# One attention and MoE kernel: the values' 16-bit parts are made in the bias stage and stored

## The chip, the core and the metric

The kernel runs on one core of a Trainium2 chip. The metric is the device time of one execution in microseconds (us). Before the change the median of three runs is 802.57 us (799.44 to 804.67).

## What is computed

Attention with a bias that comes from a small network on positions, then a gated feed-forward layer without routing ("MoE" in the code) on its output:

```python
scores = scale * np.matmul(q, k.transpose(0, 1, 3, 2))      # 4 batches, 8 heads, 576 x 576, head_dim 64
x = (log1p(|i - j|) / log1p(max(i, 1)))[..., None]
bias = np.maximum(x @ w1 + b1, 0.0) @ w2                     # 32 hidden, one bias per head
attn = softmax(scores + bias)
x = np.matmul(attn, v)  as [2304 tokens, 512]
out = (sigmoid(x @ w_gate) * (x @ w_val)) @ w_out            # d_ff 1536
```

All inputs and outputs are float32. The kernel keeps the accuracy with products of parts: a number is written as a high part and the rest, and a product as two or three matmuls of parts.

## The kernel before

**Bias stage** (`bias`, some 14 to 112 us). The bias is made per chunk of 64 query columns, nine chunks `c`. TensorE sums switches (`ind`, `far`) times coefficients into `bps` (L427); each chunk has five blocks of rows in the order `BORD` = 0, 1, 4, 2, 3, called groups here, number `5c + n`. `leave` takes a group out of PSUM: VectorE multiplies one half by `xt` into `btmp` (L435, L448), ScalarE copies the other half to `brest` for blocks 0 and 4 (L438), and the sum is made by VectorE (L443) or, for blocks 0 and 4, by GpSimd (L443, L453). `btmp`, `brest` and `bps` have two buffers each. The switches of the next chunk are made meanwhile: TensorE's L403 from a loaded table `lt` and ScalarE's L408, and VectorE's comparison L421, whose operands both lie in SBUF. VectorE and ScalarE also reformat weights for the MoE (`conv`, L225 to L237: load of `cvw`, store of `cvm`).

For the attention the values `v` are split to two 16-bit parts after a scaling by a power of two. The scale comes from the sum of squares of `v`: per batch a load of `vb` on GpSimd's queue (L458), 20 matmuls (`gram`, L350) in block 4 of chunks 3 to 6, two VectorE operations; and in chunk 7 one `fit` for all batches (L364 to L378), nine small VectorE operations and a matmul.

**Attention** (`attention`, some 110 to 372 us). There are 16 units `u`, one for a pair of heads `p` and a batch `b`. A unit has nine slots `s`. In even slots TensorE makes the scores of two tiles (L627; slot 8: one tile, L616), VectorE adds the bias and takes the minimum (L643, `mn`), ScalarE takes the exponential (`en`, L648). Two slots later (`LAG`) a tile is turned: those of head 0 by TensorE (L672, L679; then ScalarE L561 and VectorE L562 write high part and rest to `at`), those of head 1 (`CROSS`) by GpSimd, which writes both parts to `cr` (L555, L666), and a transposing DMA (L667), which is issued `XLAG` = 3 slots after. `cr` has three buffers. The last columns are turned by `tail` in slot 3 of the next unit. In each unit's slots 0 to 8 TensorE also does 0, 6, 3, 6, 3, 6, 3, 6, 3 matmuls (`FILL`) of the last unit's `products`, from slot 2 on: four groups of nine matmuls (L732), one for each head `h` and half `e` of the query columns, into the one buffer of `acc`; ScalarE copies a group to `xe` (L736), of which there are two, and when both halves of a head are there, SP stores it to `xs` (L741). `split_v` makes the two parts of the values in slots 5 and 7: ScalarE L602 and VectorE L603 on `vr`, which SP loaded (L548). VectorE's L696 scales the softmax sums for a store to `rs`.

The order of the instructions on each engine is that in which the program writes them: both stages run under a manual schedule. Each engine, and each DMA queue (almost all of it SP's), works in that order; an instruction that waits holds up those behind it.

**MoE** (`Moe`, from 372 us on, with loads and conversions in the last units of the attention). The change does not touch it.

## Time and profile before

| | |
|---|---|
| median of three runs | 802.57 us |
| the profiled execution, its own time | 800.84 us |
| its span, first to last instruction | 799.0 us |
| granted TensorE clock, mean | 0.987 of full speed |
| busy share TensorE / VectorE / ScalarE / GpSimd | 92% / 81% / 70% / 45% |
| bias stage, attention, MoE (from the trace, roughly) | 14 to 112, 110 to 372, 372 to 799 us |

In the trace PE is TensorE (PEld its weight loads), DVE VectorE, ACT ScalarE, POOL GpSimd, SPq and ACTq DMA queues. L732 is line 732 of the kernel's file. "x12" counts instructions, "<-" in a tile name reads "written from", and behind a row stands the engine's idle time before it and what ended that.

### The profile page before, as it was taken

The numbers are of one execution on the slowest core, as the hardware profiler recorded it, in microseconds if no ns is written. First come the engines' busy times: TensorE is split into PE (matmuls) and PEld (weight loads), VectorE is DVE, ScalarE is ACT, GpSimd is POOL, SyncE is SP. The second block draws the span as 40 slices with busy tenths as digits, with TensorE's granted clock in tenths as the row PEclk, the third lists the DMA queues.
The fourth block names the chain that finished last, engine by engine and source line by source line (L and its number), as shares of the span: only waits on it lengthen the run. The fifth ranks groups of instructions, "written<-read, shape, count | busy, mean of one in ns | idle before, by whom it ended". The sixth has DMA issues, their size and how long they took to land. (4 is left out here: it accounts for less than half of the span.)

```text
span 799.0 us, 17293 instructions
## 1 busy us (share of the span) xinstructions
PE 735.8 (92%) x6343; PEld 539.5 (68%) x6343; DVE 650.3 (81%) x1362; ACT 555.4 (70%) x1206; POOL 360.1 (45%) x451
## 2 busy tenths in 40 slices
PE   7999879888888988777999999998999999999997
PEld 4898867666766766565899899974555555555553
DVE  6788879888888889996498998878988886877762
ACT  5888738787887878776666666577666667666652
POOL 2245349788879986973001110046733221533100
PEclk9999988999999999999999999999999999999999
DMA  5487315878888798898989863357522211422102
GB/s 199 149 202 175 116 59 119 190 181 168 178 174 186 184 185 208 204 220 207 320 259 257 260 172 107 108 148 190 175 80 80 80 53 57 155 80 80 54 1 80
DMA packets 137237, 121.86 MB, mean 153 GB/s; under 512 B 82368, under 2 KB 106048, under 8 KB 137152
## 3 DMA queue, kind: packets, MB, share of 16 engines
...
## 5 line engine op out<-in xcount | busy, mean ns | idle before, releaser
L1158 PEld LDWEIGHTS <-wv 128*128 128x128 f16 x1008 | 98.0, 98 | 85.5 <-issue 10.7
L648 ACT ACTIVATE en<-en,mn 128x576 f32<-128x576 f32 x144 | 110.8, 774 | 24.7 <-DVE mn L643 22.6
L1116 POOL TENSOR_TENSOR ws<-wm 128x256 f32<-128x256 f32 x44 | 42.4, 964 | 157.2 <-DMA wm<-scratch 109.0
L1158 PE MATMUL pg<-xq,wv 128*128 128x384 f16 x576 | 109.3, 326 | 3.3 <-ACT c L1184 2.4
L643 DVE CUSTOM_DVE_ANT_0 en<-sc,bias 128x576 f32<-128x576 f32 x128 | 91.9, 755 | 21.5 <-PE sc L627 19.1
L732 PE MATMUL acc<-at,vv 128*128 128x288 f16 x540 | 84.1, 288 | 19.4 <-DVE at L562 10.7
L666 POOL TENSOR_TENSOR cr<-en,cr 128x512 f16<-128x512 f32 (+1 forms) x128 | 97.1, 779 | 5.3
L627 PEld LDWEIGHTS sc<-k,part 64*128 64x128 f32 x768 | 58.5, 189 | 43.1 <-DVE mn L643 16.5
L627 PE MATMUL sc<-k,part 64*128 64x288 f32 x768 | 78.3, 317 | 10.0 <-DVE mn L643 8.1
L1005 PE MATMUL po<-wo,gh 128*128 128x512 f16 x288 | 85.7, 379 | 0.0
L1158 PE MATMUL pu<-xq,wv 128*128 128x384 f16 x432 | 82.0, 326 | 2.1 <-DVE c L1164 2.1
...
L1164 DVE TENSOR_TENSOR c<-pu,c 128x384 f32<-128x384 f32 x72 | 40.0, 555 | 42.5 <-PE pu L1158 28.7
L562 DVE SCALAR_TENSOR_TENSOR at<-pt,at 128x512 f16<-128x512 f32 (+3 forms) x128 | 69.5, 564 | 5.8 <-ACT at L561 4.8
L561 ACT ACTIVATE at<-pt 128x512 f16<-128x512 f32 (+3 forms) x128 | 60.1, 496 | 19.9 <-PE pt L672 19.8
L732 PEld LDWEIGHTS <-vv 128*128 128x128 f16 x576 | 56.2, 98 | 25.0 <-issue 9.3
L427 PE MATMUL bps<-cfs,ind 128*128 128x64 bf16 x1458 | 67.5, 193 | 3.5 <-DVE bias L443 1.8
L408 ACT ACTIVATE ind<-y 128x576 bf16<-128x576 f32 x100 | 62.4, 651 | 10.8 <-PE y L403 8.0
L427 PEld LDWEIGHTS <-ind 128*128 128x128 bf16 x1458 | 58.7, 98 | 9.7 <-issue 3.0
L555 POOL TENSOR_SCALAR cr<-en 128x576 f16<-128x576 f32 x64 | 45.3, 708 | 43.9 <-DMA at<-cr 32.8
L1176 ACT ACTIVATE gh<-c 128x384 f16<-128x384 f32 x48 | 25.1, 523 | 54.1 <-DVE c L1174 52.5
L672 PE MATMUL pt<-ident,en 128*128 128x128 f32 x320 | 53.3, 291 | 6.5 <-ACT en L648 6.4
...
## 6 DMA issues: line engine op xcount, KB each, us to landing
...
```

Source lines behind the costliest of these rows:

```text
L408: nc.scalar.activation(out=o, in_=y[:, :, 0:HF], func=AF.Sigmoid, scale=float(2.0 ** 64))
L427: nc.tensor.matmul(out=o, lhsT=st, rhs=cfs[:, part], start=(part == 0), stop=(part == 2))
L561: nc.scalar.activation(out=hi, in_=ps, func=AF.Copy, scale=float(2.0 ** UP))
L562: return lambda: nc.vector.scalar_tensor_tensor(out=lo, in0=ps, scalar=float(2.0 ** UP), in1=hi, op0=ALU.mult, op1=ALU.subtract)
L627: nc.tensor.matmul(out=pair[h][:, e, 0:HF], lhsT=qs[rows, l, 128 * it:128 * it + 128], rhs=ks[rows, r, HF * e:HF * e + HF], start=(i == 0) ...
L643: nc.vector.tensor_tensor_reduce(out=half(en), in0=ps[:, :, 0:HF], in1=half(nbias), scale=-0.125, scalar=3.0e38, op0=ALU.add, op1=ALU.min, ...
L648: nc.scalar.activation(out=en, in_=en, func=AF.Exp, bias=mn, scale=-1.0, accum_out=sm)
L666: nc.gpsimd.tensor_tensor(out=t[:, a:a + z.stop - z.start], in0=en[:, z], in1=t[:, z], op=ALU.subtract)
L672: nc.tensor.transpose(pt[:, J], en[:, 128 * J:128 * J + 128], ident)
L732: nc.tensor.matmul(out=acc[:, 0:HF], lhsT=l, rhs=r, start=(i == 0), stop=(i == len(mms) - 1))
L1005: self.nc.tensor.matmul(out=po, lhsT=l[:, tt], rhs=r, start=(first and i == 0), stop=(last and i == 2))
L1158: nc.tensor.matmul(out=p, lhsT=W[i][:, l, at + kc], rhs=V[b][:, r, kc], start=(new and n == 0), stop=(n == 5), skip_group_check=not new)
```

## The change

The values' parts are made in the bias stage, by GpSimd, and stored in DRAM (`vs`, one tensor per unit); the attention loads them ready-made (`vv`, in slot 2). The scale is now one per batch. `vb` is loaded from the start on, `gram` stands in block 4 of chunks 0 to 3, and a `fit` for the batch of the chunk before in chunks 1 to 4. From group 8 on (chunk 1, fourth group) `parts` and its `rest` are called in turn, once per group: scale in place and round to the high part, then the low part by subtraction, the store of `vs` and the load of the next `vr` but one on SP. `split_v` leaves the attention. The scaling of the softmax sums moves from VectorE to ScalarE. `products` runs over column halves outside and heads inside; `cr` has four buffers; the transposing DMA is issued two slots after the turn instead of three.

```diff
-LAG, WSTEP, VSTEP, TAIL = 2, 2, (5, 7), 3
+LAG, WSTEP, VSTEP, TAIL = 2, 2, 2, 3
...
-XLAG = 3
+XLAG = 2
...
-VCHUNK = (3, 4, 5, 6, 7)
+VSTART = 7
...
+    vs = [dram.tile([128, 2, 5, 2, D], F16, name=f"vs{i}") for i in range(B * NP)]
...
+        rp, op = pool("vraw", 2), pool("vparts", 2)
         squares = cp.tile([128, B], F32, name="vsq")
...
+        most = cp.tile([128, B], BF16, name="vmost")
+        size = [level.tile([128, B], F32, name=n) for n in ("vnorm", "vup", "vun", "vout")]
+        sizes.update(out=size[3], tiny=sm[:, 2 * HID + 17 + H:2 * HID + 26 + H])
+        vb, vr, ready = [], [], []
+        nc.gpsimd.memset(ones, 1.0)
...
+        def load_vr(n):
+            t = rp.tile([128, 2, 5, D], F32, name="vr")
+            nc.sync.dma_start(out=t, in_=v[n // NP, n % NP])
+            vr.append(t)
...
+                nc.vector.tensor_copy(out=most[:, n:n + 1], in_=squares[:, n:n + 1])
...
+        def fit(ps, n):
+
...
+            a = slice(n, n + 1)
+            o = ps.rearrange("p a h j -> p (a h j)")[:, 128:129]
+            nc.tensor.matmul(out=o, lhsT=ones, rhs=most[:, a], start=True, stop=True, skip_group_check=True)
...
             def leave():
-                m, up, un = (t.bitcast(I32) for t in size[0:3])
+                m, up, un = (t[:, a].bitcast(I32) for t in size[0:3])
                 e = nc.vector
-                e.tensor_scalar(out=size[0], in0=o, scalar1=float(2.0 ** -80), scalar2=None, op0=ALU.max)
...
-                e.tensor_tensor(out=size[3], in0=size[2], in1=sm[:, 2 * HID + 26 + H:], op=ALU.mult)
+                e.tensor_tensor(out=size[3][:, a], in0=size[2][:, a], in1=sm[:, 2 * HID + 26 + H:], op=ALU.mult)
...
+        def parts(n):
+
...
+            b, p = divmod(n, NP)
+            t, o = vr.pop(0), op.tile([128, 2, 5, 2, D], F16, name="vparts")
+            hi, lo = o[:, :, :, 0], o[:, :, :, 1]
+            nc.gpsimd.tensor_scalar(out=t, in0=t, scalar1=size[1][:, b:b + 1], scalar2=1.0, op0=ALU.mult, op1=ALU.mult)
+            nc.gpsimd.tensor_scalar(out=hi, in0=t, scalar1=1.0, scalar2=1.0, op0=ALU.mult, op1=ALU.mult)
+
+            def rest():
+                nc.gpsimd.tensor_tensor(out=lo, in0=t, in1=hi, op=ALU.subtract)
+                nc.sync.dma_start(out=vs[B * p + b], in_=o)
+                if n + 2 < B * NP:
+                    load_vr(n + 2)
+
+            return rest
+
+        for n in range(2):
+            load_vb(n)
...
-                late = None
-                if blk == 4 and c in VCHUNK:
-                    at = VCHUNK.index(c)
-                    late = gram(ps[:, 1], at) if at < B else fit(ps[:, 1])
-                    if at + 1 < B:
-                        load_vb(at + 1)
-                if blk == 4 and c == VCHUNK[0] - 1:
-                    load_vb(0)
+                late = []
+                if blk == 4 and c < B:
+                    late.append(gram(ps[:, 1], c))
+                    if c + 2 < B:
+                        load_vb(c + 2)
+                if blk == 4 and 0 < c <= B:
+                    late.append(fit(ps[:, 1], c - 1))
                 leave(ps, c, blk)
-                if late:
-                    late()
+                for f in late:
+                    f()
+                if (c, n) == (0, 4):
+                    for i in range(2):
+                        load_vr(i)
+                z = 5 * c + n - VSTART - 1
+                if ready:
+                    ready.pop()()
+                elif 0 <= z and z // 2 < B * NP:
+                    ready.append(parts(z // 2))
...
-    def load_v(u):
-        p, b = units[u]
-        vraw[u] = raw.tile([128, 2, 5, D], F32, name="vr")
-        nc.sync.dma_start(out=vraw[u], in_=v[b, p])
...
-    crp = pool("crp", 3)
+    crp = pool("crp", 4)
...
-    def split_v(u, h):
-        if h == 0:
-            vsplit[u] = vp.tile([128, 2, 5, 2, D], F16, name="vv")
-        t, vv = vraw[u][:, h], vsplit[u][:, h]
-        nc.scalar.activation(out=vv[:, :, 0], in_=t, func=AF.Copy, scale=sizes["up"])
-        return lambda: nc.vector.scalar_tensor_tensor(out=vv[:, :, 1], in0=t, scalar=sizes["up"], in1=vv[:, :, 0], op0=ALU.mult, op1=ALU.subtract)
+    def load_v(u):
+        vsplit[u] = vp.tile([128, 2, 5, 2, D], F16, name="vv")
+        nc.sync.dma_start(out=vsplit[u], in_=vs[u])
...
-            nc.vector.tensor_scalar(out=rt, in0=pt[0:9, 2], scalar1=sizes["out"][0:9], scalar2=None, op0=ALU.mult)
+            nc.scalar.activation(out=rt, in_=pt[0:9, 2], func=AF.Copy, scale=sizes["out"][0:9, b:b + 1])
...
-        for h in range(2):
-            xe = xep.tile([128, S], F32, name="xe")
-            for e in range(2):
-                cs = slice(HF * e, HF * e + HF)
+        xes, pairs = {}, {}
+        for e in range(2):
+            cs = slice(HF * e, HF * e + HF)
+            for h in range(2):
+                if e == 0:
+                    xes[h] = xep.tile([128, S], F32, name="xe")
+                xe = xes[h]
                 if u < NU - 1:
                     acc = ps_v.tile([128, 512], F32, name="acc")
                 else:
                     if e == 0:
-                        pair = ps_s.tile([128, 2, 512], F32, name="sc")
-                    acc = pair[:, e]
+                        pairs[h] = ps_s.tile([128, 2, 512], F32, name="sc")
+                    acc = pairs[h][:, e]
                 vv = vsplit[u][:, h]
...
-            if s in VSTEP and u < NU:
-                late.append(split_v(u, VSTEP.index(s)))
-                if s == VSTEP[1] and u + 1 < NU:
-                    loads.append(lambda z=u + 1: load_v(z))
+            if s == VSTEP and u < NU:
+                loads.append(lambda z=u: load_v(z))
```

GpSimd's rows from chunk 3 to chunk 4 of the bias stage, before (`vb` is the values in bfloat16, `biasL`, `bias` and `btmp`, `brest` as above):

```order
L443 TENSOR_TENSOR bias_72<-brest,btmp 128x2x6x32
L443 TENSOR_TENSOR bias_73<-brest,btmp 128x2x2x32
L458 DMA vb<-in_v_dram 128x4x640
L453 TENSOR_TENSOR biasL<-brest,btmp 64x4x32 x4
L443 TENSOR_TENSOR bias_72<-brest,btmp 128x2x6x32
L443 TENSOR_TENSOR bias_73<-brest,btmp 128x2x2x32
```

and after, from one block-0 addition to the next (lines are those of the new file: L474 and L484 are the additions, L402, L403 and L406 the parts):

```order
L474 TENSOR_TENSOR bias_88<-brest,btmp 128x2x6x32
L474 TENSOR_TENSOR bias_89<-brest,btmp 128x2x2x32
L406 TENSOR_TENSOR vparts<-vr,vparts 128x10x64
L402 TENSOR_SCALAR vr<-vr,vup 128x640
L403 TENSOR_SCALAR vparts<-vr 128x10x64
L484 TENSOR_TENSOR biasL<-brest,btmp 64x4x32 x4
L406 TENSOR_TENSOR vparts<-vr,vparts 128x10x64
L402 TENSOR_SCALAR vr<-vr,vup 128x640
L403 TENSOR_SCALAR vparts<-vr 128x10x64
L406 TENSOR_TENSOR vparts<-vr,vparts 128x10x64
L474 TENSOR_TENSOR bias_88<-brest,btmp 128x2x6x32
```

Three half-parts more stand between an addition for block 4 and the next for block 0, two between that one and the next for block 4.

VectorE's rows around slots 7 and 8 of a middle unit, before:

```order
L647 TENSOR_SCALAR mn<-mn 128x1
L603 SCALAR_TENSOR_TENSOR vv<-vr,vup,vv 128x5x64
L562 SCALAR_TENSOR_TENSOR at<-pt,at 128x4x128
L643 ISA en,mn<-sc,biasL 128x576
L643 ISA mn 128x1
L603 SCALAR_TENSOR_TENSOR vv<-vr,vup,vv 128x5x64
L562 SCALAR_TENSOR_TENSOR at<-pt,at 128x4x128
L562 SCALAR_TENSOR_TENSOR at<-pt,at 64x512
L643 ISA en,mn<-sc,bias_72 128x576
```

and after (L671, L589 and L667 are L647, L562 and L643 of before):

```order
L671 TENSOR_SCALAR mn<-mn 128x1
L589 SCALAR_TENSOR_TENSOR at<-pt,at 128x4x128
L667 ISA en,mn<-sc,biasL 128x576
L667 ISA mn 128x1
L589 SCALAR_TENSOR_TENSOR at<-pt,at 128x4x128
L589 SCALAR_TENSOR_TENSOR at<-pt,at 64x512
L667 ISA en,mn<-sc,bias_88 128x576
```

The two splits of the values are gone from between the minima.

ScalarE's rows from slot 4 to slot 8 of unit 2, before (L561 with 64x2x64 is the high part of the tail, `xe` the copy of a product group):

```order
L561 ACTIVATE at_3430<-pt_3700 64x2x64
L736 ACTIVATE xe_3691<-acc_3692 128x288
L561 ACTIVATE at_3675<-pt_3732 128x4x128
L648 ACTIVATE en_3728,sm_3604<-en_3728,mn_3729 128x576
L648 ACTIVATE en_3730,sm_3604<-en_3730,mn_3731 128x576
L736 ACTIVATE xe_3691<-acc_3750 128x288
L602 ACTIVATE vv_3769<-vr_3629,vup_181 128x5x64
```

and after (L588, L672, L763 are L561, L648, L736; L720 is the scaling of the sums):

```order
L588 ACTIVATE at_3825<-pt_3851 64x2x64
L763 ACTIVATE xe_3842<-acc_3843 128x288
L588 ACTIVATE at_3825<-pt_3882 128x4x128
L672 ACTIVATE en_3878,sm_3756<-en_3878,mn_3879 128x576
L672 ACTIVATE en_3880,sm_3756<-en_3880,mn_3881 128x576
L720 ACTIVATE rt_3854<-pt_3851,vout_206 9x128
L763 ACTIVATE xe_3902<-acc_3903 128x288
```

The second group goes to the other `xe`: it is head 1's first half now, no longer head 0's second.

## Rows read from the trace of the kernel before

**Rows 1.** The page: busy us (share of the span) and instructions of each engine.

```profile
PE 735.8 (92%) x6343; PEld 539.5 (68%) x6343; DVE 650.3 (81%) x1362; ACT 555.4 (70%) x1206; POOL 360.1 (45%) x451
```

**Rows 2.** Windows, MoE: us, busy PE PEld DVE ACT POOL, clock, DMA share, GB/s.

```profile
400.00:799.00 399.00, 388.00 (x2112) 258.74 (x2111) 317.19 (x549) 252.45 (x511) 109.85 (x120) 1.00 0.41 124
```

**Rows 3.** Windows: sum and mean over 12 units of the attention, 126.56 to 309.81 us.

```profile
sum 183.25, PE 161.94 PEld 125.68 DVE 162.58 ACT 149.51 POOL 153.93; mean PE 13.50 PEld 10.47 DVE 13.55 ACT 12.46 POOL 12.83
```

**Rows 4.** Windows: sum over the last three units, 309.81 to 372.30 us.

```profile
sum 62.49, PE 46.72 PEld 34.71 DVE 54.71 ACT 46.28 POOL 45.08; mean PE 15.57 PEld 11.57 DVE 18.24 ACT 15.43 POOL 15.03
```

**Rows 5.** Windows: one chunk of the bias stage, and the sum over six.

```profile
71.25:83.57 12.32, 10.71 (x267) 9.89 (x263) 9.79 (x22) 9.63 (x17) 6.88 (x9) 1.00 0.77 182
...
sum 65.96, PE 62.49 PEld 57.54 DVE 55.78 ACT 53.66 POOL 27.02; mean PE 10.41 PEld 9.59 DVE 9.30 ACT 8.94 POOL 4.50
```

**Rows 6.** Waits of PE, the same 12 units: us in total, times, longest.

```profile
PE acc L732 <- DVE at L562: 6.9, 12, 0.6
PE sc L627 <- DVE mn L643: 6.5, 18, 0.8
PE pt L672 <- ACT en L648: 4.5, 10, 0.6
PE acc L732 <- ACT xe L736: 3.2, 11, 0.3
```

**Rows 7.** Lines by form, DVE, 12 units: count | busy us, mean ns | idle before.

```profile
L643 DVE CUSTOM_DVE_ANT_0 en<-sc,bias 128x576 f32<-128x576 f32 x96 | 68.9, 755 | 17.1 <-PE sc L627 14.8 <-POOL k L566 1.1 <-POOL cr L666 0.6
...
L603 DVE SCALAR_TENSOR_TENSOR vv<-vr,vup,vv 128x320 f16<-128x320 f32 x25 | 21.6, 865 | 0.5
...
L696 DVE TENSOR_SCALAR rt<-pt,vout 9x128 f32<-9x128 f32 x12 | 4.1, 339 | 0.4
```

**Rows 8.** Lines by form, ACT, the same 12 units.

```profile
L602 ACT ACTIVATE vv<-vr,vup 128x320 f16<-128x320 f32 x24 | 13.3, 553 | 0.0
```

**Rows 9.** Lines by form, DVE, the last three units.

```profile
L603 DVE SCALAR_TENSOR_TENSOR vv<-vr,vup,vv 128x320 f16<-128x320 f32 x7 | 6.3, 903 | 0.0
```

**Rows 10.** Waits of PE, the last three units.

```profile
PE acc L732 <- DVE at L562: 3.8, 3, 2.7
PE sc L732 <- DVE at L562: 3.1, 2, 2.9
```

**Rows 11.** Lines by form, POOL, 12 units of the attention.

```profile
L666 POOL TENSOR_TENSOR cr<-en,cr 128x512 f16<-128x512 f32 x47 | 55.5, 1181 | 3.9
L555 POOL TENSOR_SCALAR cr<-en 128x576 f16<-128x576 f32 x48 | 33.2, 691 | 23.6 <-DMA at<-cr 19.6 <-ACT en L648 2.9 <-ACT xe L736 1.1
L566 POOL TENSOR_TENSOR part<-qr,part 128x640 fp32r<-128x640 f32 x12 | 18.6, 1553 | 1.0
...
L555 POOL TENSOR_SCALAR part<-qr 128x640 fp32r<-128x640 f32 x12 | 8.7, 725 | 0.0
```

**Rows 12.** Lines by form, POOL, bias stage.

```profile
L458 POOL DMA_DIRECT2D vb<-in_v_dram x4 | 3.4, 850 | 0.0
```

**Rows 13.** Timeline of one unit: start us, us, engine, line, operation, tiles.

```profile
200.24 0.56 DVE L603 SCALAR_TENSOR_TENSOR vv<-vr,vup,vv 128x320 f16<-128x320 f32 x1
...
202.07 0.66 POOL L555 TENSOR_SCALAR cr<-en 128x576 f16<-128x576 f32 x1
202.14 0.93 DVE L603 SCALAR_TENSOR_TENSOR vv<-vr,vup,vv 128x320 f16<-128x320 f32 x1
```

**Rows 14.** Tile `cr`: count, duration in ns (min/median/max), first and last start.

```profile
L555 POOL TENSOR_SCALAR cr<-en x64: 661/671/980, 117.4 to 368.9; 128x576 f16<-128x576 f32 x64
```

**Rows 15.** Timeline of DVE at the end of the bias stage.

```profile
106.84 1.63 DVE L237 SCALAR_TENSOR_TENSOR cvm<-cvw,cvm 128x512 int32<-128x512 int32 x1
...
110.89 0.69 DVE L435 TENSOR_TENSOR btmp<-bps,xt 128x512 f32<-128x512 f32 x1 [0.70 <-POOL biasL L453]
```

**Rows 16.** Lines by form, DVE, bias stage.

```profile
L421 DVE TENSOR_TENSOR far<-dist,edge 128x1024 bf16<-128x1024 f16 x16 | 10.9, 684 | 0.0
...
L237 DVE SCALAR_TENSOR_TENSOR cvm<-cvw,cvm 128x512 int32<-128x512 int32 x9 | 7.1, 787 | 0.0
...
L373 DVE TENSOR_SCALAR vnorm<-vnorm 128x1 int32<-128x1 int32 x1 | 0.2, 154 | 0.0
```

30 lines of the change are left out of this document (10 added, 20 removed).

## The prediction

> **What bounds the kernel now.** I read the page first: TensorE is busy for 92% of the span, VectorE for 81% [rows 1]. That is a mean over three stages, so I cut the span into windows. The last half is the MoE, where TensorE is busy 388.0 of 399 us [rows 2]; the change does not touch it and it is left as it is. The two stages that are touched have slack on TensorE. A middle unit of the attention (one of 16 pairs of heads and batch) takes 183.25/12 = 15.27 us, with TensorE busy 13.50, VectorE 13.55, ScalarE 12.46 and GpSimd 12.83 [rows 3]: nobody is full, all four are near it. The last three units share their time with preparations for the MoE and take 62.49 us, VectorE 54.71 of them [rows 4]. In the bias stage one chunk (of nine) takes 65.96/6 = 10.99 us, with TensorE 10.41, VectorE 9.30 and GpSimd 4.50 [rows 5]. So GpSimd has 6.5 us of room per chunk, VectorE 1.7, TensorE 0.6.
>
> Then the waits of TensorE in the attention. In 12 units it stood 6.9 us for `at` from VectorE (L562), 6.5 for `mn` (L643), 4.5 for `en` from ScalarE and 3.2 for `xe` [rows 6], 21.1 us in all. The first is one wait per unit of 0.6 us: the last matmul of the second product group (h=0, e=1) reads the columns that `tail` has just transposed, and VectorE has not split them yet. The second and third come from VectorE being late with its queue.
>
> **The change, part by part (attention).** What leaves VectorE: per unit two splits of the values (L603, 865 ns each) and one scaling (L696, 339 ns) [rows 7], 2.07 us of 13.55. What leaves ScalarE: two copies of 553 ns [rows 8]; the scaling of the sums arrives there, for which I take VectorE's 0.34 us: 0.77 us less. The load of `vv` has the bytes of the load of `vr` and takes its place on the queue. The new order of the products puts the group that reads the tail third instead of second, some 3 us later, so the first wait goes: 6.9 us. Of the second and third I take half, (6.5+4.5)/2 = 5.5, because with 2.07 us less in front of it `mn` comes earlier, but the scores still need two minima after each pair of tiles. That is 12.4 us in 12 units, 1.03 each, and 13.4 for units 0 to 12. Bounds: the first wait alone, 7.5; all four, 22.9.
>
> In the last three units VectorE sheds 6.3 us of L603 [rows 9] and four L696, 1.4 us [rows 7], 7.7 in all, and TensorE waits 3.8 + 3.1 us for `at` [rows 10]. I take 5, near the middle of 2 and 7.7. Sum of the attention: 18.4 us gained, bounds 9.5 and 30.6.
>
> The fourth `cr` buffer and the lag of 2 remove GpSimd's waits for a buffer (19.6 us of L555 in 12 units [rows 11]). I price that at nothing: GpSimd's work there is hidden under the scores of the next tiles. If it isn't, the gain is inside the upper bound. Group (h=1, e=0) moves forward to slot 4 and needs a transposing DMA that is issued at slot 0, four slots or some 7 us ahead; late, it would cost up to 1 us per unit.
>
> **The change, part by part (bias stage).** Sixteen times GpSimd now scales 128x640, rounds it to 16 bits and subtracts. The trace of before has no such instructions, but near ones: one input, 128x640, 725 ns; `cr`, one input to 16 bits, 691 ns for 576 columns, so 0.77 for 640; two inputs to 16 bits, 1181 ns for 512, so 1.48 [rows 11]. With three gaps of 0.08 one part is 3.2 us, 51 us in all. They go in at five half-parts per chunk, from the fourth group of chunk 1 to the end of chunk 7: 2.5 x 3.2 = 8.0 us. GpSimd's old work per chunk is 4.50 less the loads of `vb`, which move to the start (3.4/6 = 0.6 [rows 12]), less the split of `qr` that falls in one of the six chunks ((0.73 + 1.55)/6 = 0.4 [rows 11]): 3.5. Sum 11.5 us per chunk, where the chunk has 10.99. GpSimd is full, and there is more.
>
> VectorE and GpSimd get in each other's way. Two L603 of one unit take 0.56 and 0.93 us; the long one started 0.07 us after a GpSimd instruction and ends 0.34 after that one's end [rows 13]. An L237 that met a GpSimd subtraction takes 1.63 us [rows 15], the mean of nine is 0.79 [rows 16]. The mean of L603, 865 ns [rows 7], is 0.31 above the short one. VectorE has five operations with both operands in SBUF per chunk (three L421, L234, L237 [rows 16]) that seldom met GpSimd so far. With GpSimd full each gets 0.4: +2.0 us. The fit per batch adds 8 small operations of 0.15 us [rows 16] in four chunks, 0.7 a chunk. VectorE: 9.30 + 2.7 = 12.0. The other way round GpSimd's L555 on `cr` takes 661 ns at least and 980 at most [rows 14]; of these 0.32 us I take a little under half, 0.14, for each such meeting: 11.5 + 0.7 = 12.2.
>
> The Trainium skill (GPSIMD Engine Reference, Engine selection and Elementwise — side-by-side cycle accounting) puts one-input work on GpSimd at about line rate and two-input work at some 2.6 cycles per element; from these figures an estimate for a part is 0.53 + 0.53 + 1.39 = 2.45 us, which would make 9.6 us a chunk, leave VectorE's 12.0 to set the pace and the forecast at 790. The rows of this case are dearer, 3.2, and decide.
>
> Two engines at 12.0 and 12.2, and TensorE at 10.41, with two buffers each for `btmp` and `brest` between them: VectorE's write of `btmp` waits for GpSimd's addition, two groups earlier, and behind it stand the evictions that TensorE waits for. I take 12.3 us a chunk, +1.3 over 6.5 chunks = 8.5. At the end of the stage the splits of `kr` and the last `biasL` additions come later; VectorE's last L435 waits 0.70 us for them already [rows 15], and the first scores wait for VectorE: +1. Bias stage: 9.5 us lost. Bounds: -1 (GpSimd runs ahead through its groups, and the 12.32 us chunk falls to the 11.0 of the others [rows 5]) and +36 (below).
>
> New waits on SP: the store of `vs` waits for the subtraction, behind it stand the next load of `vr`, the loads of `lt` (for L403) and the weights (for L225). It is hidden as long as GpSimd is under a group late: `lt` is loaded a chunk ahead. At the start two `vb` loads share the DMA engines with `xt` and the second `lt`; TensorE's first matmuls need neither, so I put nothing, and 1 us as the bound.
>
> **Sum.** 800.84 (the profiled execution: span 799.0) - 18.4 + 9.5 = 791.9. The median of the runs shown, 802.57, is 1.7 above that execution. I predict 792.
>
> **Rivals.**
> *The lock is whole on both sides* (chance 0.15). Each of the five VectorE operations stops GpSimd for its full 0.68 us: 11.5 + 3.4 = 14.9 a chunk, +3.9 x 6.5 + 1 = 26.4, time 808.8. For: [rows 13, 15]. Against: no L555 on `cr` is delayed by more than 0.32. The Trainium skill (SBUF — State Buffer, Who interferes with whom) says this: two SBUF inputs contend with a GpSimd read, and the second to issue fully blocks. VectorE's side of it the trace shows.
>
> *GpSimd's parts are dear* (0.09; the other side). If scaling by a per-partition value, or writing every second block of 64, costs as much as a two-input instruction (1.55 for 128x640 [rows 11]), a part is 4.9 us: 3.5 + 12.2 + 0.7 = 16.4 a chunk, +5.4 x 6.5 + 1 = 36, time 818. It decides (over 810.6) from 4.4 us a part; at 3.8 the gain is eaten. For: no row of that form. Against: the one-input rows, to 32 and to 16 bits, cost 0.73 and 0.69.
>
> *VectorE is not what the scores wait for* (0.15). Only the lower bound of the attention comes, 9.5: time 800.8. For: the chain scores, minimum, scores has two L643 of 755 ns [rows 7] per pair of tiles, which stay.
>
> *The bias stage hides it* (0.16): -18.4 - 1, time 781. For: additions are needed only two groups later, so GpSimd may be a little late unseen. Against: 11.5 of 10.99.
>
> **Chances.** The forecast, 786 to 797, has 0.45. About 1% (8 us) is what a measurement of this kernel can tell from no change: faster is below 794.5, slower above 810.6. Faster: 0.16 + four fifths of 0.45 + 0.03 of the third rival = 0.55. Slower: the dear parts and 0.01 of the lock = 0.10. The same: 0.35. A range of 780 to 807 holds the forecast, the third rival, most of the fourth and half of the lock: 0.8.
>
> **What would show it.** Right: no wait of the products for `at`; a middle unit of 14.2 us; GpSimd near 100% and chunks of 12.3 us from 30 to 105 us; L421 means above 0.9 us. Wrong: a part under 2.7 or over 4 us; middle units at 15; products waiting for the transposes; chunks at 11.

## The result, and the profile after

The changed kernel takes 809.45 us in the median of ten runs (807.76 to 812.71), the kernel before 804.12 in ten runs beside it; the ratio is 1.0074, with a 95% interval of 1.005 to 1.0099. It is slower by an amount that can be told from zero, but within the 1% named in the prediction: no change by that bound, where a gain of 1.3% was forecast. The profiled execution has a span of 805.9 us, 6.9 more than before. The page gives the span, and busy time by engine beside [rows 1]:

```profile
span 805.9 us, 17337 instructions
...
PE 738.9 (92%) x6346; PEld 542.5 (67%) x6346; DVE 637.9 (79%) x1337; ACT 545.6 (68%) x1190; POOL 409.4 (51%) x499
```

Further down, medians are over all runs of a kernel and ratios over those that were not slow as a whole (left out are one run of no_parts, one of parts_set and two of one_split). The page alone hides what happened: VectorE lost 12 us of work and GpSimd gained 49. By stage:

| stretch | before | after | difference | forecast |
|---|---|---|---|---|
| start to the first scores | 110.35 | 133.39 | +23.0 | +9.5 |
| units 0 to 12 of the attention | 199.46 | 180.54 | -18.9 | -13.4 |
| unit 13 to the end (three units, MoE) | 489.2 | 492.0 | +2.8 | -5 |

Lines have moved: the scores are L651 (L627 before), the products L759 (L732), the additions of the bias L474 (L443), `far` L452 (L421), the narrowed weights `cvm` L226 to L238 (L225 to L237). The windows of units 1 to 12, to be read beside [rows 3], and TensorE's waits in them, beside [rows 6]:

```profile
sum 166.17, PE 160.01 PEld 124.78 DVE 143.05 ACT 143.13 POOL 152.13; mean PE 13.33 PEld 10.40 DVE 11.92 ACT 11.93 POOL 12.68
```
```profile
PE acc L759 <- ACT xe L763: 3.2, 11, 0.4
...
PE sc L651 <- DVE mn L667: 0.6, 2, 0.3
...
PE pt L696 <- ACT en L672: 0.5, 1, 0.5
```

A unit takes 166.17/12 = 13.85 us with TensorE busy 13.33: TensorE sets it now. Its waits for `at` are gone, and of those for `mn` and `en`, 11.0 us together, 1.1 are left. The gain is more than was forecast (14.2 us a unit).

The bias stage, two of its chunks and six with their sum, beside [rows 5]:

```profile
44.48:58.93 14.45, 11.91 (x249) 10.70 (x249) 12.01 (x30) 8.69 (x16) 12.17 (x14) 0.88 0.72 240
...
86.34:101.56 15.22, 12.24 (x231) 10.66 (x231) 13.85 (x20) 9.72 (x18) 14.62 (x17) 0.78 0.62 212
...
sum 83.92, PE 67.86 PEld 60.55 DVE 74.53 ACT 56.54 POOL 71.89; mean PE 11.31 PEld 10.09 DVE 12.42 ACT 9.42 POOL 11.98
```

A chunk takes 13.99 us, where 10.99 was the mean before. In the five chunks from 44.48 on it is 14.19, with GpSimd busy 12.85 and VectorE 12.76, so neither is full. TensorE's granted clock is 0.78 and 0.88 in the two chunks shown, so for part of them it ran at the lower of its two levels, and its busy time there is the longer for it; in the same stretch of no_parts, below, it is 1.00 throughout. The chunk is not long because of it: in late_store_vb, below, the clock is 1.00 in all five chunks and they still take 14.04 us. Counted at GpSimd's first addition to `bias` in each chunk, 2.9 of the 23.0 us lie in chunk 0 (14.18 us for 11.26), 18.0 in the six chunks and 2.0 behind them.

What TensorE and ScalarE wait for between 28 us and the first scores (us in total, times, longest); then, from 14 to 134 us, what GpSimd waits for at the load of `vb`; then SP's own queue from 28 to 134 us:

```profile
PE y L434 <- ACT ind L439: 11.7, 10, 3.5
...
PE bps L458 <- DVE bias L474: 8.5, 11, 1.9
...
ACT cvm L226 <- DMA cvw<-in_moe_w_out_dram: 7.2, 2, 3.9
...
PE bps L458 <- ACT brest L469: 4.2, 3, 1.8
...
ACT cvm L226 <- DMA cvw<-in_moe_w_val_dram: 2.7, 2, 2.0
ACT cvm L226 <- DMA cvw<-in_moe_w_gate_dram: 2.7, 1, 2.7
```
```profile
POOL vb L350 <- PE y L434: 8.7, 2, 6.4
```
```profile
SPq L407 <- POOL vparts L406: 72.7, 16, 16.1
```

Three waits are new. SP stands 72.7 us at the stores of `vs`, each of which waits for a subtraction on GpSimd (its queue stood before too, 39.1 us at the stores of `cvm`, without ScalarE waiting); the weights `cvw` are behind them on the queue, and ScalarE, in order, waits 12.6 us for these (0.4 in the same stretch before); TensorE waits 11.7 us for ScalarE's switches (3.0 before). GpSimd stands at the load of `vb`, whose buffer is freed by the sums of squares of the very same group, and `biasL` is behind it. And VectorE's `bias` is late (8.5; 1.4 before).

Operations of both engines by form, 28 to 115.44 us (count | busy us, mean ns | idle before), and one meeting in the timeline (start us, us):

```profile
L452 DVE TENSOR_TENSOR far<-dist,edge 128x1024 bf16<-128x1024 f16 x14 | 16.2, 1157 | 0.0
...
L235 DVE SCALAR_TENSOR_TENSOR cvm<-cvw,cvm 128x512 int32<-128x512 int32 x8 | 7.7, 964 | 0.0
L229 DVE TENSOR_SCALAR cvm<-cvm 128x512 f32<-128x512 f32 x8 | 6.0, 750 | 0.0
```
```profile
L406 POOL TENSOR_TENSOR vparts<-vr,vparts 128x640 f16<-128x640 f32 x13 | 19.4, 1490 | 0.9
L402 POOL TENSOR_SCALAR vr<-vr,vup 128x640 f32<-128x640 f32 x14 | 15.8, 1131 | 0.4
...
L403 POOL TENSOR_SCALAR vparts<-vr 128x640 f16<-128x640 f32 x14 | 11.3, 810 | 1.2
```
```profile
93.50 1.40 POOL L406 TENSOR_TENSOR vparts<-vr,vparts 128x640 f16<-128x640 f32 x1
93.56 1.88 DVE L235 SCALAR_TENSOR_TENSOR cvm<-cvw,cvm 128x512 int32<-128x512 int32 x1
...
94.88 1.23 POOL L402 TENSOR_SCALAR vr<-vr,vup 128x640 f32<-128x640 f32 x1
```

A part costs GpSimd 1.13 + 0.81 + 1.49 = 3.43 us, near the forecast 3.2. `far` takes 1157 ns where it took 684 [rows 16]. In the timeline L235 starts 0.06 us behind GpSimd's subtraction and goes on to 0.54 us past its end, 1.88 us in place of some 0.7; and the GpSimd instruction that follows is drawn out in turn, 1.23 us.

The last three units take 66.16 us (62.49 before [rows 4]):

```profile
313.93:336.46 22.53, 16.22 (x117) 12.05 (x116) 15.10 (x37) 12.83 (x34) 17.98 (x21) 0.77 1.05 239
```

In unit 13 the DMA engines are full (share 1.05; 0.93 before, when the unit took 19.29 us), and TensorE waits up to 5.9 us at a time for a transpose.

### The profile page after: what moved, and what is told of

The parts are those of the page before. It is cut to its first block, busy times and chain, and to the rows that moved or that the text cites. A ratio compares the mean times of both kernels' runs of the same rounds, so it can differ in the third digit from the quotient of the medians.

```text
span 805.9 us, 17337 instructions
## 1 busy us (share of the span) xinstructions
PE 738.9 (92%) x6346; PEld 542.5 (67%) x6346; DVE 637.9 (79%) x1337; ACT 545.6 (68%) x1190; POOL 409.4 (51%) x499
## 5 line engine op out<-in xcount | busy, mean ns | idle before, releaser
L672 ACT ACTIVATE en<-en,mn 128x576 f32<-128x576 f32 x144 | 110.8, 774 | 16.9 <-DVE mn L667 15.1
L667 DVE CUSTOM_DVE_ANT_0 en<-sc,bias 128x576 f32<-128x576 f32 x128 | 91.8, 754 | 19.5 <-PE sc L651 18.5
L690 POOL TENSOR_TENSOR cr<-en,cr 128x512 f16<-128x512 f32 (+1 forms) x128 | 92.2, 742 | 5.3
L759 PE MATMUL acc<-at,vv 128*128 128x288 f16 x540 | 82.3, 290 | 13.5 <-ACT xe L763 6.8
L759 PEld LDWEIGHTS <-vv 128*128 128x128 f16 x576 | 57.4, 100 | 37.5 <-issue 18.1
L458 PE MATMUL bps<-cfs,ind 128*128 128x64 bf16 x1458 | 69.8, 196 | 12.8 <-DVE bias L474 8.5
L651 PE MATMUL sc<-k,part 64*128 64x288 f32 x768 | 77.7, 319 | 3.1 <-DVE mn L667 1.6
L589 DVE SCALAR_TENSOR_TENSOR at<-pt,at 128x512 f16<-128x512 f32 (+3 forms) x128 | 70.1, 568 | 13.1 <-ACT at L588 11.6
L458 PEld LDWEIGHTS <-ind 128*128 128x128 bf16 x1458 | 60.8, 100 | 20.2 <-DVE bias L474 8.3
L651 PEld LDWEIGHTS sc<-k,part 64*128 64x128 f32 x768 | 58.7, 191 | 22.1 <-issue 11.4
L588 ACT ACTIVATE at<-pt 128x512 f16<-128x512 f32 (+3 forms) x128 | 60.3, 497 | 15.9 <-PE pt L696 13.9
L434 PE MATMUL y<-lt,wy 128*128 128x288 bf16 x204 | 44.0, 302 | 14.6 <-ACT ind L439 12.2
L1006 PE MATMUL pg<-xhi,w 128*128 128x384 f32 x192 | 54.4, 341 | 1.1 <-ACT g L1015 0.9
```

Of the source, the lines that this page charges most:

```text
L458: nc.tensor.matmul(out=o, lhsT=st, rhs=cfs[:, part], start=(part == 0), stop=(part == 2))
L588: nc.scalar.activation(out=hi, in_=ps, func=AF.Copy, scale=float(2.0 ** UP))
L589: return lambda: nc.vector.scalar_tensor_tensor(out=lo, in0=ps, scalar=float(2.0 ** UP), in1=hi, op0=ALU.mult, op1=ALU.subtract)
L651: nc.tensor.matmul(out=pair[h][:, e, 0:HF], lhsT=qs[rows, l, 128 * it:128 * it + 128], rhs=ks[rows, r, HF * e:HF * e + HF], start=(i == 0) ...
L667: nc.vector.tensor_tensor_reduce(out=half(en), in0=ps[:, :, 0:HF], in1=half(nbias), scale=-0.125, scalar=3.0e38, op0=ALU.add, op1=ALU.min, ...
L672: nc.scalar.activation(out=en, in_=en, func=AF.Exp, bias=mn, scale=-1.0, accum_out=sm)
```

## The experiments

Eighteen kernels were run. What each gave, with the first scores (start of the first L651 or what answers to it), the mean of units 1 to 12, and the time from the start of unit 13 to the end, all read from its trace; the ratio is to runs of the kernel before on the same chip. The three stage columns are of one execution each, so a difference of 1 or 2 us in them can be chance (the ten runs of the changed kernel lie within 5 us):

```
run            first scores  unit  13 to end   median us  ratio (95% interval)
before            110.4     15.27    489.2      804.12
after             133.4     13.85    492.0      809.45   1.0074 (1.0050 to 1.0099)
no_parts          116.2     13.84    492.0      790.39   0.9823 (0.9781 to 0.9865)
no_parts_vb       112.6     13.82    489.9      787.18   0.9810 (0.9786 to 0.9835)
half_width        124.1     13.81    491.1      797.07   0.9932 (0.9905 to 0.9959)
half_late         118.8     13.81    491.0      791.34   0.9850 (0.9815 to 0.9885)
parts_set         123.2     13.84    488.6      797.78   0.9921 (0.9889 to 0.9952)
halves            141.0     13.82    488.2      809.85   1.0080 (1.0055 to 1.0105)
vb_late           134.8     13.84    489.2      807.80   1.0047 (1.0017 to 1.0076)
deep4             136.1     13.80    490.1      806.77   1.0020 (0.9995 to 1.0044)
deep_vb           135.4     13.81    489.6      806.37   0.9999 (0.9972 to 1.0027)
late_store        132.4     13.85    489.8      803.25   0.9997 (0.9976 to 1.0018)
late_store_vb     126.6     13.85    490.2      799.19   0.9945 (0.9917 to 0.9972)
parts_va_vb       129.0     13.85    491.0      804.56   0.9998 (0.9976 to 1.0019)
xlag3             133.5     13.98    490.5      808.26   1.0072 (1.0048 to 1.0096)
order_all         110.1     15.21    488.6      800.93   0.9971 (0.9945 to 0.9997)
values_only       135.4     15.09    489.7      821.73   1.0224 (1.0187 to 1.0261)
one_split         109.9     15.67    491.7      803.02   0.9949 (0.9912 to 0.9987)
split_order       110.3     14.36    489.3      789.51   0.9840 (0.9813 to 0.9866)
split_early       110.3     14.72    490.6      797.42   0.9906 (0.9884 to 0.9929)
```

### What the parts cost in the bias stage

**no_parts.** The work on GpSimd left out:

```diff
+        blank = op.tile([128, 2, 5, 2, D], F16, name="vparts")
+        nc.gpsimd.memset(blank, 0.01)
...
-            t, o = vr.pop(0), op.tile([128, 2, 5, 2, D], F16, name="vparts")
...
-            nc.gpsimd.tensor_scalar(out=t, ...); nc.gpsimd.tensor_scalar(out=hi, ...)
+            t, o = vr.pop(0), blank
...
-                nc.gpsimd.tensor_tensor(out=lo, in0=t, in1=hi, op=ALU.subtract)
```

> The changed kernel without the three GpSimd instructions per part: a constant tile is stored to `vs` in their place, so the values are not those of the reference; loads, stores, gram and fit stay. Theory A (GpSimd's new work, and VectorE's waits behind it, make the 14.0 us chunks): chunks 1 to 7 fall back to 11 to 11.5 us, the first scores come 16 to 19 us earlier than at 133.4, the time is about 792. Rival B (the added transfers and SP's new waits make them): chunks stay near 14, the time is within 3 us of the changed kernel's.

As theory A has it: first scores at 116.2, 17.2 us earlier, 790.4 us. Loads and stores stayed, so the transfers by themselves (the first half of rival B) are not what costs. The second half is not tested here: a constant tile is ready at once, so SP's waits for a subtraction went together with GpSimd's work. TensorE's wait for the switches is back at its old size, and `far` at its old length (44 to 104 us):

```profile
PE y L433 <- ACT ind L438: 3.0, 8, 0.8
```
```profile
L451 DVE TENSOR_TENSOR far<-dist,edge 128x1024 bf16<-128x1024 f16 x12 | 8.2, 683 | 0.0
```

**half_width.** Half of that work:

```diff
+        blank = [op.tile([128, 2, 5, 2, D], F16, name="vparts") for _ in range(2)]
+        for t in blank:
+            nc.gpsimd.memset(t, 0.01)
...
-            t, o = vr.pop(0), op.tile([128, 2, 5, 2, D], F16, name="vparts")
-            hi, lo = o[:, :, :, 0], o[:, :, :, 1]
+            t, o = vr.pop(0)[:, 0], blank[n % 2]
+            hi, lo = o[:, 0, :, 0], o[:, 0, :, 1]
```

> The changed kernel with the three GpSimd instructions of each part done for the first of two heads only (128x320), the other half being a constant: GpSimd's parts fall from 3.4 to about 2.0 us, its load from 12.8 to about 9.2 us per chunk, well under the chunk's 11.0. The step of the prediction (the chunk is as long as the fullest engine): VectorE at 11.0 to 11.5 sets the pace, chunks 2 to 6 take 11.5 or less and the first scores come at 117 or earlier (116.2 without parts). Rival J (every us put on GpSimd delays what stands behind it in queues of two buffers, full or not): about half of the way, chunks 12.5 to 13, first scores at 123 to 126.

Rival J: 124.1, half of the way, although GpSimd is busy only 8.4 of 11 us. So "the chunk is as long as the fullest engine" fails. (Two constant tiles are set first here. Counted from GpSimd's first addition to `bias`, the first scores come after 104.13 us, where it is 116.05 in the changed kernel and 97.95 in no_parts: a third of the cost is still there for half of the work.) ScalarE still waits 9.4 us for weights, in three rows (12.6 in the changed kernel), which is what half_late later took away:

```profile
PE y L438 <- ACT ind L443: 10.3, 10, 2.9
...
ACT cvm L226 <- DMA cvw<-in_moe_w_out_dram: 3.5, 2, 2.1
ACT cvm L226 <- DMA cvw<-in_moe_w_gate_dram: 3.5, 1, 3.5
...
ACT cvm L226 <- DMA cvw<-in_moe_w_val_dram: 2.4, 1, 2.4
```

**parts_set.** The three instructions become memsets:

```diff
+            nc.gpsimd.memset(t, 0.01)
+            nc.gpsimd.memset(o[:, :, :, 0], 0.01)
...
+                nc.gpsimd.memset(o, 0.01)
```

> The changed kernel with the three GpSimd instructions per part replaced by three memsets of the same three tiles (fp32 128x640, 16-bit 128x640, 16-bit 128x1280), so GpSimd is about as long at work but reads nothing from SBUF; the stored values are constants. Theory A1 (VectorE's operations wait for GpSimd instructions that read SBUF): L452 falls from 1.36 us to 0.69 at 128x1024, chunks to about 12, the time to about 798. A2 (GpSimd being full is enough): L452 falls, but chunks stay above 13.3, time about 806. A3 (any GpSimd access blocks): L452 stays above 1.1 us, time about 808.

The memsets take 2.5 us a part, less than 3.4, so the time is no clean price; the operations are. (The 1.36 us of the expectation is not the mean from 28 to 115 us shown above, 1157 ns.) The timeline, two places:

```profile
76.57 1.17 POOL L405 MEMSET vparts<- 128x1280 f16 x1
...
77.24 0.68 DVE L235 SCALAR_TENSOR_TENSOR cvm<-cvw,cvm 128x512 int32<-128x512 int32 x1
```
```profile
81.55 1.16 POOL L405 MEMSET vparts<- 128x1280 f16 x1
...
81.64 2.49 DVE L229 TENSOR_SCALAR cvm<-cvm 128x512 f32<-128x512 f32 x1
...
82.65 0.62 POOL L401 MEMSET vr<- 128x640 f32 x1
...
83.22 0.62 POOL L402 MEMSET vparts<- 128x640 f16 x1
```

Operations with two SBUF operands no longer wait (L235 0.68 us; `far` 716 ns in the mean): A1. But L229, with one operand, waits for three memsets in a row, 2.49 us in place of 0.42. The Trainium skill (SBUF — State Buffer, Who interferes with whom) tells both apart: two SBUF inputs contend with a GpSimd instruction that reads, not with one that only writes; a `tensor_scalar` in a two-port mode contends with GpSimd, and whoever issues second blocks fully. The rows of L235 and `far` agree; those of L229 do if it runs in such a mode, which the trace does not show.

**halves.** Each instruction as two of half the width, as the last here:

```diff
-                nc.gpsimd.tensor_tensor(out=lo, in0=t, in1=hi, op=ALU.subtract)
+                for x in range(2):
+                    nc.gpsimd.tensor_tensor(out=lo[:, x], in0=t[:, x], in1=hi[:, x], op=ALU.subtract)
```

> The changed kernel with each of the three GpSimd instructions of a part issued as two of half the width; same result, same work, two more fixed costs per instruction pair. Theory F (a VectorE operation that starts under a GpSimd instruction waits for the end of that one instruction): the mean of L452 at 128x1024 falls from 1.16 us to about 0.95, VectorE's busy time per chunk falls by about 0.8 us, while GpSimd's parts grow from 3.4 to about 3.9 us, so the time changes by less than 3 us either way. Rival G (VectorE waits as long as GpSimd has work): L452 stays at 1.1 or more and the time grows by 4 us or more.

F for the operations: `far` falls to 963 ns, so an operation waits for the one instruction. Not for the stage: GpSimd's parts grew to 4.3 us and the first scores came at 141.0. Five chunks of 15.16 us, GpSimd busy 14.61 in each, VectorE 11.87:

```profile
sum 75.80, PE 59.66 PEld 53.37 DVE 59.36 ACT 46.90 POOL 73.03; mean PE 11.93 PEld 10.67 DVE 11.87 ACT 9.38 POOL 14.61
```

Here GpSimd, busy for 96% of the time, sets the pace of the chunks; the queues are worse too (ScalarE waits 19.8 us for weights). (The median is that of the changed kernel all the same. The span of its profiled execution, 809.7, is only 3.8 us longer, although the first scores come 7.6 us later, since its time from unit 13 on is the shortest of all.)

**parts_va_vb.** The parts by ScalarE and VectorE, and the `vb` loads moved as in vb_late:

```diff
-            nc.gpsimd.tensor_scalar(out=t, ...); nc.gpsimd.tensor_scalar(out=hi, ...)
+            nc.scalar.activation(out=hi, in_=t, func=AF.Copy, scale=size[1][:, b:b + 1])
...
-                nc.gpsimd.tensor_tensor(out=lo, in0=t, in1=hi, op=ALU.subtract)
+                nc.vector.scalar_tensor_tensor(out=lo, in0=t, scalar=size[1][:, b:b + 1], in1=hi, op0=ALU.mult, op1=ALU.subtract)
```

> The changed kernel with the parts still made in the bias stage, but by ScalarE (scale and round, one instruction of 128x640) and VectorE (one scale-and-subtract of 128x640), GpSimd none; and the loads of `vb` 2 and 3 issued in the next chunk. Theory A (GpSimd's length and the waits of VectorE behind it made the 14.0 us chunks): L452 is back at 0.69 us, VectorE 9.3 + 0.7 + 2.5 x 0.9 = 12.2 us per chunk, ScalarE 10.9, chunks 12.0 to 12.4, first scores near 120, the time 794 to 797. Rival H (any 16 parts in this stage cost what they did, since VectorE is the tighter engine): chunks 13.5 or more, the time 805 or more.

Rival H. With GpSimd at a third, chunks 2 to 6 take 68.40/5 = 13.7 us with VectorE busy 11.89 and ScalarE 10.47: the work is now in the queues of the two engines that TensorE waits for most directly. Taking GpSimd out of it does not make the stage free. SP's queue is not cleared of blame here: it still stands 54.9 us at the stores, now for VectorE, though ScalarE waits only 1.5 us for weights; a run with late stores as well was not made.

### Queues and buffers

**vb_late.** The load leaves the group of `gram(c)`:

```diff
-                    if c + 2 < B:
-                        load_vb(c + 2)
...
+                if n == 1 and 1 <= c and c + 1 < B:
+                    load_vb(c + 1)
```

> The changed kernel with the loads of `vb` 2 and 3 issued in the second group of the next chunk, when their buffer has long been free, not in the group whose own products free it. Theory C (in chunks 0 and 1 GpSimd stands at this load and holds back the additions to `biasL`, for which VectorE and then TensorE wait): the wait of GpSimd for `y` at the load goes, chunk 0 falls from 14.2 to 11.3 us and chunk 1 by 1 to 2, the first scores come 4 us earlier, time 805. Rival: that wait is hidden behind the parts' later delay, chunk 0 falls but the first scores stay within 1 us of 133.4, time 809.

The rival: chunk 0 falls from 14.2 to 11.8 us, the first scores come at 134.8; what is gained is lost in later chunks. **no_parts_vb**, the same without the parts, shows the price where nothing hides it:

> The changed kernel without the GpSimd instructions of the parts (a constant tile is stored) and with the loads of `vb` 2 and 3 issued in the next chunk. Theory C2 (the 5.9 us by which the first scores still come late without parts, 116.2 against 110.3, are GpSimd's wait for the products of its own group): first scores at 112 or 113, chunks 0 and 1 at 11 to 12 us, the time about 787. Rival: the rest is the fit per batch and the transfers: first scores at 115 or later, the time about 790.

112.6, so 3.6 us is what GpSimd's wait at this load costs where no parts are made (C2).

**deep4** and (with the late loads) **deep_vb**:

```diff
-        tp = pool("bt", 2)
+        tp = pool("bt", 4)
```

> The changed kernel with four buffers in place of two for `btmp` and `brest` in the bias stage, nothing else. Theory L (a late addition on GpSimd stops VectorE by its buffer): VectorE no longer waits for `biasL` or `bias` of GpSimd, GpSimd may run late, chunks 2 to 6 fall from 14.2 to GpSimd's own 12.8, first scores at 124 to 127, the time about 801. Rival M (VectorE's operations that wait for GpSimd instructions are what counts): L452 stays at 1.1 us or more and chunks at 13.7 or more, first scores after 131, the time 807 to 811.

> deep4 with the loads of `vb` 2 and 3 issued in the next chunk as well. If theory L holds, the gain of 3 to 4 us in chunk 0 is no longer lost later: first scores at 121 to 124, the time about 798. If M holds: as vb_late, first scores after 131, the time 806 to 809.

Rival M both times: 136.1 and 135.4, `far` at 1213 and 1024 ns. The buffers of `btmp` and `brest` are not what couples the engines.

**late_store** and **late_store_vb.** SP's queue freed; the store is put off by two groups:

```diff
-        rp, op = pool("vraw", 2), pool("vparts", 2)
+        rp, op = pool("vraw", 3), pool("vparts", 3)
...
-                nc.sync.dma_start(out=vs[B * p + b], in_=o)
+                while done:
+                    done.pop()()
+                done.append(lambda: nc.sync.dma_start(out=vs[B * p + b], in_=o))
...
```

> The changed kernel with each store of `vs` issued two groups later, when its subtraction is done, and three buffers for the raw values and for the parts, so that the loads of `vr` need not wait either; GpSimd's and VectorE's work is unchanged. Theory P (SP's queue stands at the stores and delays the weights that ScalarE needs in order): SP's waits for the subtraction fall from 72.7 us to under 15, ScalarE's waits for `cvw` from 12.6 to under 2, TensorE's for `ind` from 11.7 to 3 or 4; the first scores come at 122 to 126, the time is about 800. Rival M (GpSimd and VectorE at 12.8 and 12.9 us per chunk are late next): those waits go, but TensorE's for VectorE's `bias` grow in their place, the first scores stay after 130, the time is 806 or more.

> late_store with the loads of `vb` 2 and 3 issued in the next chunk as well. Theory P: without parts this move was worth 3.6 us in first scores (116.2 to 112.6), with SP's queue free it is worth that here too: first scores at 119 to 123, the time about 797. Rival M: first scores within 1.5 us of late_store's.

In late_store SP still waits at the store (49.5 us, where under 15 was expected), but with less harm: ScalarE's waits for `cvw` fall from 12.6 to 2.5 us and TensorE's for the switches from 11.7 to 5.8. Alone this gives 1 us of first scores (rival M), as vb_late alone gave none; the time falls by more, 6 us in the median, of which the traces, 3.3 us apart, show 2.1 from unit 13 on. Together the two give 6.8 us of first scores, and the time falls by 10 to 799.2. In late_store_vb five chunks, one of them and their sum, take 70.20 us:

```profile
83.60:99.30 15.70, 13.05 (x316) 11.49 (x316) 15.56 (x25) 12.94 (x24) 15.10 (x16) 1.00 0.66 209
...
sum 70.20, PE 54.94 PEld 48.81 DVE 66.81 ACT 47.35 POOL 67.04; mean PE 10.99 PEld 9.76 DVE 13.36 ACT 9.47 POOL 13.41
```

VectorE and GpSimd are both busy for 95% of the 14.04 us. That the two meet more now, and that the meetings fill the time, is in part shown: for the same instructions and one load of `vb` more (0.8 us) GpSimd is busy 13.4 us a chunk in place of 12.85. The windows hold not quite the same instructions of VectorE; over the same 122 of them, in chunks 2 to 6, it is busy 9.78 us a chunk in no_parts, 12.25 in the changed kernel and 12.47 here. At GpSimd's additions these five chunks are hardly shorter than in the changed kernel (14.04 for 14.19). Of the 6.8 us, 2.4 come in chunk 0 and 4.4 behind chunk 6, where the first scores follow after 13.6 us in place of 17.9.

**half_late** puts half_width on top of that:

> half_width with the stores of `vs` two groups later, three buffers for the raw values and the parts, and the loads of `vb` 2 and 3 in the next chunk: GpSimd does the parts of the first of two heads only, the other half is a constant. Theory Q (where no engine is full, the loss is the queues: SP's at the stores, GpSimd's at the loads of `vb`): ScalarE's waits for `cvw` under 3 us, chunks 2 to 6 at 11.0 to 11.5 us, first scores at 114 to 117 (124.1 in half_width, 112.6 without parts and with late `vb`), the time about 789. Rival R (VectorE's waits for GpSimd instructions cost the chunk at any load): chunks at 12 or more, first scores after 120, the time 794 or more.

Between the two: ScalarE's waits for `cvw` are gone and TensorE's for the switches are 2.9 us. The first scores come at 118.8, and 2.6 us of it is this kernel's own start (three constant tiles are set first: GpSimd's first addition to `bias` is at 20.8 us, at 18.2 in no_parts_vb). Counted from that addition it is 97.95 us, 104.13 in half_width and 94.38 in no_parts_vb. So of the 9.75 us that half the work cost, 6.2 were the queues and 3.6 GpSimd's own work and the meetings.

### The attention

**order_all** puts the new loops of `products`, four `cr` buffers and the lag of 2 on the kernel before; **values_only** takes the same three from the changed kernel:

```diff
-        for h in range(2):
-            for e in range(2):
+        for e in range(2):
+            for h in range(2):
...
-    crp = pool("crp", 3)
+    crp = pool("crp", 4)
...
-XLAG = 3
+XLAG = 2
```

> The kernel before with only the new order of products, four `cr` buffers and the lag of 2; the values are split in the attention as before. Theory D (the order is what shortens the unit; VectorE's 2.1 us of splits are the smaller part): units 1 to 12 fall from 15.27 to 14.1 to 14.4 us, first scores stay at 110.4, the time is about 792. Rival E (VectorE's load sets the unit): units stay at 14.9 or more, time 799 to 803.

> The changed kernel with the old order of products (both column halves of a head in turn), three `cr` buffers and the lag of 3; the values still come ready split from `vs`. Theory E (VectorE's 2.1 us of splits and scaling set the unit, the order is worth nothing): units 1 to 12 take 13.8 to 13.9 us as in the changed kernel, the last three units 62 to 64 us (66.2 in the changed kernel), first scores stay near 133.4, the time is 806 to 810. Rival D2 (with the splits gone the wait for `at` in the second product group comes back): units take 14.3 to 14.5 us, the time is 814 to 817.

Each is the miss of one view. With order, buffers and lag alone units take 15.21 us: the wait for `at` is gone, and TensorE waits about as much longer for VectorE's minimum (12.5 us in eleven units, 6.5 in twelve before), with VectorE at 13.67:

```profile
sum 182.50, PE 164.38 PEld 127.79 DVE 163.99 ACT 148.43 POOL 156.95; mean PE 13.70 PEld 10.65 DVE 13.67 ACT 12.37 POOL 13.08
```
```profile
PE sc L627 <- DVE mn L643: 12.5, 30, 0.8
```

With the values alone units 1 to 6 take 14.40 us (the wait for `at` is there again, 3.8 us in six units), and units 8 to 12, from 249.4 to 329.7 us, 14.2 to 18.1, when TensorE and GpSimd wait 6.6 and 9.0 us for the transposes. TensorE's wait in the first stretch, and both in the second:

```profile
PE acc L756 <- DVE at L589: 3.8, 6, 0.9
```
```profile
POOL cr L582 <- DMA at<-cr: 9.0, 4, 3.5
...
PE acc L756 <- DMA at<-cr: 6.6, 3, 3.2
```

Together they give 13.85. The terms do not add: order, buffers and lag 0.06, values 0.18 (0.9 in the first six units), both 1.42 us a unit.

**xlag3**, the lag alone undone on the changed kernel:

```diff
-XLAG = 2
+XLAG = 3
```

> The changed kernel with the transposes again issued with the lag of 3, four `cr` buffers and the new order kept. Theory K (the lag of 2 is needed since group (h=1, e=0) is one slot earlier): TensorE waits for `at` from the transposes in the middle units, units 14.1 or more, the time 813 or more. Rival (the transposes land 4 slots ahead anyway): units stay at 13.8, the time within 2 us of 809.5; if the stall of unit 13 (22.5 us) then falls to that of before (19.3), it is the early lag that made it.

The rival: the twelve units take 13.98 us in the mean, 13.8 to 13.9 each but for the first, 15.7, so the lag is not what made the difference. The new order and the fourth buffer were not tried apart. Unit 13 still takes 21.7 us; the early lag does not make its stall.

**one_split**, on the kernel before, one split per unit:

```diff
-        t, vv = vraw[u][:, h], vsplit[u][:, h]
+        t, vv = vraw[u], vsplit[u]
...
-            nc.vector.tensor_scalar(out=rt, in0=pt[0:9, 2], scalar1=sizes["out"][0:9], scalar2=None, op0=ALU.mult)
+            nc.scalar.activation(out=rt, in_=pt[0:9, 2], func=AF.Copy, scale=sizes["out"][0:9])
```

> The kernel before with the values of a unit split by one instruction of 128x640 on ScalarE and one on VectorE in place of two of 128x320 each, and the scaling of the sums on ScalarE. VectorE is spared one fixed cost, one meeting with GpSimd and 0.34 us: 0.8 us of 13.55 per unit. Theory E (VectorE's load sets the unit, 1.43 us of period for 1.75 us of load): units 15.27 - 0.65 = 14.6 us, time 803.7 - 13 x 0.65 = 795. Rival: units stay at 15.2, the time within 2 us of before.

Between theory and rival by itself: 0.5%, with runs from 794.6 to 807.8 us. The profiled one is the longest of the ten, so its units of 15.67 us, and the 10.0 us that GpSimd waits for transposes in it from 217 to 278 us, do not stand for the median. **split_order** adds the new order, four buffers and the lag of 2:

> Both of the last findings together: the kernel before with the new order of products, four `cr` buffers and the lag of 2, and with the values of a unit split in the attention by one instruction on ScalarE and one on VectorE, the scaling of the sums on ScalarE; nothing of the values in the bias stage but the sums of squares as before. Theory E2 (with the order's waits gone VectorE's load sets the unit: 1.4 us of period for the 1.8 us of load that the changed kernel sheds): VectorE is spared 0.8 us of 13.7, units 15.25 - 0.65 = 14.6 us, first scores at 110, the time 800.9 - 13 x 0.65 = 792.5. Rival: the load that counts is the meeting with GpSimd, which stays: units 15.1 or more, the time 799 or more.

This beats both kernels: 789.51 us, ratio 0.984. The bias stage is that of before (110.3), units take 14.36 us:

```profile
sum 172.20, PE 165.43 PEld 126.16 DVE 157.44 ACT 149.79 POOL 159.88; mean PE 13.79 PEld 10.51 DVE 13.12 ACT 12.48 POOL 13.32
```
```profile
L602 DVE SCALAR_TENSOR_TENSOR vv<-vr,vup,vv 128x640 f16<-128x640 f32 x12 | 17.7, 1477 | 0.0
```

**split_early** moves the split within the unit:

```diff
-LAG, WSTEP, VSTEP, TAIL = 2, 2, (5, 7), 3
+LAG, WSTEP, VSTEP, TAIL = 2, 2, (0, 7), 3
```

> The kernel of split_order with the split of the values moved from slot 5 to slot 0 of the unit, where GpSimd has a gap of 0.8 us. Theory N (the meeting with GpSimd, 1.48 us for VectorE's operation of 0.89, lengthens the unit): the operation falls to about 0.9 us, units from 14.1 to 14.5 down to 13.9, the time 789.5 - 13 x 0.4 = 784. Rival: other work is late next (the scores' two minima), units stay at 14.1 or more, the time within 2 us of 789.5.

Half of N: the operation falls to 885 ns, but it now stands in VectorE's queue waiting for ScalarE, and the next wait is TensorE's for `xe`, which ScalarE evicts late; units 14.72 us, the kernel 1% slower than split_order:

```profile
L602 DVE SCALAR_TENSOR_TENSOR vv<-vr,vup,vv 128x640 f16<-128x640 f32 x12 | 10.6, 885 | 12.8 <-ACT vv L601 12.8
```
```profile
PE acc L734 <- ACT xe L738: 11.7, 11, 1.1
```

## Why the prediction was wrong

**Attention, units 0 to 12: direction right, size and working not.** 18.9 us were gained where 13.4 was forecast, inside the bounds. But the sum took the wait for `at` (6.9 us) as the order's gain and half of the others as VectorE's. order_all and values_only show that they are limits behind one another: with one of them gone the other holds the unit, at 15.2 us, or at 14.4 in the first six units and more later. "I take half" undersized the last step: with both gone TensorE waits 4.3 us in 12 units, where it waited 21.1. The fourth buffer and the lag, "priced at nothing", may be part of it: values_only, without them and the order, has GpSimd and TensorE waiting for transposes in its later units. No run has the buffer alone.

**Last three units: wrong.** The step "I take 5, near the middle of 2 and 7.7" failed. The kernels of the table, whose VectorE sheds nothing, part or all of the splits, take 488.2 to 492.0 us from the start of unit 13 to the end. What VectorE sheds there does not reach the end. In unit 13 TensorE waits for transposes on full DMA engines; what fixes the sum of the three units and the MoE stays open.

**Bias stage: +23.0 for +9.5, the step that decides.** GpSimd's part was well priced (3.43 for 3.2). Five things failed.
- The overlap. The two engines' sums were 12.0 and 12.2, and 12.3 was taken as the larger of them, as if each were busy while the other is, with 0.1 us for all waits. The sums were the smaller miss: GpSimd is busy 12.85 us a chunk, and VectorE 12.25 over the instructions counted above. The chunk takes 14.19 with neither full, and with the queue waits eased (late_store_vb) 14.04, with GpSimd busy 13.4. From 126.6 against 112.6, the work with its meetings costs 14.0 us, where 9.5 was forecast. How much of that is GpSimd's length and how much the meetings no run separates.
- The meetings. In the mean their price was near: `far` took 0.47 us more, 0.4 was assumed, and VectorE's instructions in all 2.5 us a chunk more than in no_parts, for 2.0. But one meeting costs a VectorE operation what is left of the GpSimd instruction, so up to 1.3 us here (the longest `far` took 2.02), and the list of five operations missed those with one operand (L229, 750 ns for 416), which meet too.
- "New waits on SP ... hidden as long as GpSimd is under a group late": this was put at nothing. SP waited 72.7 us at the stores, and ScalarE 12.6 us for weights behind them.
- The load of `vb` was counted as 0.6 us taken off GpSimd's chunk, without the wait that comes with it: its buffer is freed in the same group. Without parts that is 3.6 us. Both queues together are 6.8 us of the 23.0.
- The remaining 112.6 - 110.4 = 2.2 us has no term of its own in the sum: nothing was put for the start. It can be the fit per batch, the sums moved to chunk 0 and the first loads; these were not taken apart, and some 0.9 of it is no_parts_vb's own start (GpSimd's first addition to `bias` is at 18.2 us, at 17.3 in the changed kernel).

**The rivals.** The whole lock gave 808.8, and 809.45 was measured, but by another sum: VectorE waits for GpSimd rather than GpSimd for VectorE (GpSimd is busy 12.85 us a chunk, not 14.9), with the two queues beside it, a larger gain in the attention and none after it. That this rival's number lies so near is luck. Neither dear parts, nor a VectorE that the scores do not wait for, nor a bias stage that hides the work came true. The estimate of 2.45 us for a part, worked out from figures of the Trainium skill (GPSIMD Engine Reference, Engine selection and Elementwise — side-by-side cycle accounting), is under the 3.43 measured beside VectorE, and under 0.79 + 0.72 + 1.40 = 2.91 from the shortest of each instruction.
